# Two gated blocks between linear-attention layers: the first gated block opens with row tiles 0 and 1 in one group, and the five engine orders are written anew

## The chip, the cores and the metric

The kernel runs as one program on one core of a Trainium2 chip. The metric is the device time of one execution in microseconds (us). Seven executions of the kernel before gave 379.11 to 379.82 us, median 379.69 us.

## The reference

The input x has 2048 rows of 512 bf16 numbers. Four blocks follow one another, each with a layer norm in front and a residual sum behind it: A (attention), B (gated), A again, B again, with the same weights in both rounds.

```
A(x):  q, k, v = x @ wqkv, 32 heads of 16
       phi(t) = [softmax(t @ w_phi), softmax(-(t @ w_phi))]   # per head, 16 + 16 features
       kv = sum over rows of phi(k)^T v ;  z = sum over rows of phi(k)
       o  = phi(q) kv / (phi(q) z + 1e-6) ;  result o @ wo
B(x):  gate = x @ W_gate ; up = x @ W_up        # 512 -> 1376
       result (relu(gate) * up) @ W_down        # 1376 -> 512
x = x + A(norm(x)); x = x + B(norm(x)); x = x + A(norm(x)); x = x + B(norm(x))
```

The sum over all rows in kv is the one place where no row can go on until every row is done. Everything else goes row tile by row tile.

## The kernel before

The rows are cut into 16 tiles of 128. x stays on chip as `x_sb`. The blocks have the tags A0, B1, A2 and B3, and the layer norms in front of them L0 to L3.

**Attention.** For a tile t the names are: `k t` and `v t` (projection matmuls, line 725, or 766 for pairs of tiles), `expk` (two exponentials on ScalarE), `Zk` (a row reduction on VectorE), `rZk` (its reciprocal), `phik` (the scaling, on GpSimd or VectorE), and `kvacc` (line 787), which adds into PSUM banks 0 and 1. After the last tile, `kvbd` and `kvf` (lines 797 and 808, VectorE) take kv out of these two banks. Then, for each tile, comes the numerator: for tiles 0 and 1, and 10 to 15, of A0, `num` is eight small matmuls (line 921), `rden` and `o` on VectorE. For tiles 2 to 9 of A0 (line 886) the eight products of 144 columns go to PSUM in three groups, `numcp t 0`, `t 1`, `t 2` evacuate them (line 413, ScalarE or VectorE), and `zm`, `zd`, `zr`, `ab`, `tsc` and `o` do the division. The three groups take banks 6 and 7 in turn. `otr` transposes `o` (on TensorE with an evacuating copy for tiles 0 and 1, by a DMA on SyncE's queue for the others). `wo t` is the output projection (line 942, four matmuls), `resid` adds it to x (line 687, VectorE), `apply` centres the row for the next norm (line 703), and `L1 tr t` transposes it into `yT` (TensorE plus copy for tiles 0 and 1, a DMA else). The query projections stand as `q 6 2` and so on (line 868: four tiles at a time, transposed) or `q 12` (line 822), each with exponentials `expq`. The exponentials of a pair of tiles are two ScalarE instructions over two banks.

**Gated block.** `glu_up` takes a group of row tiles `ts` and walks over 11 chunks of the 1376 columns. For each of ten full chunks, `Wg` and `Wu` (line 962) make four matmuls each: the weights' chunk stands in the array, and `yT` of the group streams through it, so that a matmul has 128 columns for each tile in the group. `relu` (line 964) brings the gate out of PSUM on ScalarE; in every second chunk `up` (line 970) brings the other product out on ScalarE too and `h` (line 972) multiplies on VectorE, in the others `h` (line 975) reads PSUM itself. The last chunk, of 96 columns, is done the other way about (`gu`, line 988, four matmuls of 192 columns for each tile, with `h` line 993) and comes first; its product goes through a DMA transpose (`htr`). The products of gate and up go round banks 0 to 3, which the query projections used before. `glu_down` (line 1011) is eleven matmuls of 512 columns per tile, and its `resid` (line 1013) adds to x.

**The order of the work.** `emit` lists the operations; each has a number. The dictionary `ORDER` holds, for each of the five engines, the numbers in base 36 in the order in which that engine runs them; nothing decides this at run time. `CHOICE` says on which engine an operation runs that more than one could do. Semaphore waits are derived from the operations' reads and writes. The durations written beside the operations only help to sort the operations when waits are shared out. SyncE issues all transposes and most weight loads in the order of its list, and an issue that waits holds up those behind it. `dummy` (line 539) stands for 70 matmuls without use, spread over the first part of TensorE's list.

In the first gated block the groups are: tile 0, tile 1, tiles 2 and 3, tiles 4 to 7, 8 to 11, 12 to 15. In the second one they are: tiles 0 and 1, tiles 2 and 3, and then the same fours.

Of the kernel before, what the change touches and what calls it, by code (L numbers as in the profile page):

```python
# [14 lines left out]
        "29 26 6 25 27 28 2a 2b 4t 2c 39 49 3u 4y 4e 44 5i 5n 58 5s 4j 6j 6k 67 73 72 8l 6d 84 6a 4o 83 8k 91 9x 9y 7r 96 9z c4 c5 9b c6 9g d9 da db b4 f9 f8 "  # L15
        "fm fl ay ee ef b2 eg gz gy fz h0 hx hw fy ij g5 g4 ik gb ga gg gh ii hv mk mj n4 n3 mu mt lm lq lt ne nd nn no nt r8 o5 o4 rf of op oq jv kn p0 pa pb "
        "vg pl pw pv vk q6 qg qh qr s1 ko sd sc sn xw xt sx sy t8 lg tt tj ti zn u4 ue u3 zu up uo uz wd wo wp x9 wz xa m8 ru ym yn xk z7 11o z8 yx 10k 11s zi "
        "10l 11v 10v 142 w2 12t yb 149 146 134 13p 135 13f 109 159 14z 13q 15a 15u 12a 15v 15k 14o 16x 178 177 17i 1b7 16m 18l 1aw 1c9 1db 1ad 1by 1d0 1e6 1dv "
        "1ea 1f0 1fg 1ew 1em 1gj 1fw 1gk 1fc 1gi 1jm 1hk 1hl 1hj 1kb 1fs 1ib 1ic 1kr 1l7 1g8 1ia 1j2 1j3 1gx 1ll 1lk 1j1 1m9 1ma 1nv 1k6 1ob 1mz 1my 1lj 1or "
        "1l3 1kn 1p7 1nn 1m8 1mn 1no 1mx 1pl 1pk 1ly 1q9 1nm 1o7 1nc 1qa 1pj 1qz 1qy 1on 1rq 1rp 1q8 1s4 1p3 1qx 1s3 1py 1ro 1t5 1t6 1s5 1s6 1t8 1qn 1t7 1u7 "  # L20
        "1ua 1u8 1xr 1uw 1uv 1u9 1xx 1y3 1uy 1ym 1yn 1ux 1z1 1z2 1y9 1yl 1zh 1zg 1z0 1zv 1zw 1zf 24t 1zu 24u 255 24v 24w 256 258 230 257 25u 25t 25h 25i 25k "
        "25w 25v 25j 26q 271 27d 272 22j 27n 27c 27z 27o 27y 289 28a 28l 28k 28v 28w 297 29h 296 29i 29t 29s 2be 23c 23x 2bp 2bq 24i 2cc 2cb 2c1 26f 2c0 2dj "
        "2cn 2cm 2di 2dt 2b3 2e5 2du 2e4 2ef 2eg 2er 2eq 2ft 2fu 2hu 2i5 2i6 2ih 2ig 2j2 2ir 2j3 2a7 2is 2d7 2kg 2k6 2kh 2k5 2l2 2l3 2ks 2kr 2mh 2le 2mg 2ld "
        "2fi 2hb 2ju 2m5 2qa 2pz 2qb 2n8 2ql 2qw 2qx 2qm 2sa 2r7 2sl 2sb 2r8 2ny 2sw 2sx 2t7 2sm 2pg 2t8 2um 2tj 2ti 2ul 2g8 2rz 2mv 2ua 2vw 2x5 2ak 2v0 2xg "
        "2xr 2xh 2od 2y3 2xs 2y2 2vd 2yd 2yp 2ye 2yo 2z0 2zb 2yz 2zm 2za 2zl 2gl 2wo 2zw 2zx 308 2wb 307 30z 2oq 31c 30m 322 "),
    "dve": (
        "2z 30 33 3a 3b 3e 3l 3m 3v 3k 3w 3p 2m 53 3z 5d 5x 5z 5t 5v 5u 60 5y 5w 7i 7g 7f 7h 6l 64 6m ao 74 ap 75 an am 85 7t 86 8m a0 7x 8n 7v a3 a1 a4 c7 ca "
        "c8 cb dc df b0 fa dg fn dd fo fb eh ek el ei em h1 h2 fq h4 hy hz h5 i1 il im i0 in io j2 j1 j3 j4 ix jd iz je iy j0 k6 jj k7 ku ky l1 l2 jo l3 l4 jp "
        "l6 l7 lv lw ju kc ly lz nu kh rc rg ki rh og ld ri o6 le or p1 rk pc pm rl vn vo q7 m5 px vq qi m6 xp qs kp s2 vs so se r4 sz xy xz t9 rr tk tu y1 u5 "
        "uf uq zr 13s we lh v0 zw zx zy zz rs vc 13t vz x0 wq w0 y8 y9 xb yo xl 13v 106 107 17w yy 15x zj 15y m9 z9 17x 15z 10m 17y 1b9 1ba 19o 10w 12u 11y 181 "  # L30
        "19p 14c 120 121 136 118 14d 13g 16c 14e 16d 150 19r 1cb 127 11k 13r 15b w3 128 1cc 18b 18c 15w 15l 1cd 14l 14m 16y 16j 16k 17j 179 17v 18i 18j 1a3 1a4 "
        "1bo 1bp 19b 1cq 1cr 18z 1aa 1ab 1b8 1dl 1ax 1dm 19n 1bv 1cx 1bw 1cy 1ca 1e8 1ds 1dt 1e7 1eb 1dc 1ey 1fe 1f3 1fh 1d1 1en 1ex 1jk 1kp 1fu 1fx 1gl 1fj "
        "1ft 12b 1k9 1fd 1l8 1ks 1gy 1dw 1hm 1g9 1hn 1j4 1j5 1gm 1id 1ha 1go 1nt 1l5 1nw 1mb 1ie 1i1 1hp 1mc 1la 1o9 1is 1k7 1jj 1p5 1oc 1gn 1os 1op 1ko 1p8 "
        "1lm 1ln 1n0 1ig 1n1 1n2 1l4 1lo 1pm 1lz 1lp 1nd 1np 1mo 1j7 1nq 1pn 1po 1r0 1pp 1r1 1o8 1r3 1qb 1qc 1s7 1s8 1oo 1p4 1rr 1rs 1se 1sf 1pz 1qo 1t9 1tg "
        "1rf 1xp 1ta 1th 1qe 201 1xs 1sw 1xv 202 203 20f 1xu 1ty 1tl 204 20g 1y1 208 209 1yo 1um 1y7 1y6 1yp 1z3 1ya 1yq 1z4 1yc 1zi 1zj 1zl 1zx 1zy 200 1zz "
        "20a 21r 21q 21s 21p 20d 221 222 227 22u 22v 22c 23n 23o 22d 20m 22i 248 249 235 236 265 23b 20n 2et 26r 266 2gm 2eu 24f 23u 23v 273 2ev 27e 2gn 280 "
        "28b 27p 2at 24g 2au 28m 2go 2lg 298 2cx 29j 28x 29u 2cy 2j5 26c 2j6 26d 2n9 2na 2f8 2f9 2bf 23d 2a6 2lh 2br 2aj 2li 2ll 2b0 2h1 2cd 2c2 2h2 2d4 2ff "
        "2co 23y 2b1 2or 2os 2dk 2nc 2d5 2fg 2e6 2eh 2dv 2es 2tl 2fv 2jk 2jl 2g7 2ra 2ou 2b4 2hv 2rb 2i7 2ow 2lv 2tm 2lw 2gk 2it 2h8 2h9 2ii 2j4 2no 2m2 2k7 "
        "2np 2rf 2m3 2jr 2js 2l4 2ki 2kt 2p6 2p7 2lf 2mi 2mu 2rp 2nv 2nw 2rq 2n7 2m6 2u0 2u1 2qc 2q0 2hc 2jv 2op 2oc 2vm 2pd 2qn 2qy 2pe 2r9 2sc 2rw 2rx 2vn "
        "2t9 2sn 2sy 2tk 2un 2uz 2u7 2u8 2vt 2vu 2vc 2x6 2xt 2ub 2xi 2wa 2yf 2wn 2y4 2yq 2s0 2zn 2z1 2zy 2zc 309 30l 30y 31b 31o 320 "),  # L40
# [375 lines left out]
class Kernel:  # L416
# [609 lines left out]
    def emit(self):  # L1026
# [45 lines left out]
        for li in (0, 2):  # L1072
# [52 lines left out]
            else:  # L1125
                for f in steps_B([0], HA):
                    f()
# [86 lines left out]
```

The softmax here doesn't subtract the row's maximum and nothing guards it: scores larger than these inputs give would overflow.

## Time and profile before

| what | value |
|---|---|
| seven executions | 379.11 to 379.82 us, median 379.69 us |
| the profiled execution's own time | 379.33 us |
| its span, first to last instruction | 377.2 us |
| TensorE busy (matmuls) | 368.0 us, 98% of the span |
| VectorE, ScalarE, GpSimd busy | 276.1, 226.9, 130.6 us |
| granted TensorE clock | 1.000 |

The time of the profiled execution is its span and 2.1 us around it. Busy time of TensorE counts a matmul from its start to its modelled end, and matmuls overlap: a 512-column matmul is shown with 379 ns, while four of them in a row take 0.86 us in the chain, a pace of 0.216 us each. So the pace, and not the mean duration, says what a matmul costs in a full queue.

### The profile page before, as it was taken

To read this page: it belongs to the slowest core of one execution; us is meant where nothing else is said; L and a number is where in the kernel's file an instruction comes from. 1 tells how busy PE (TensorE), PEld (TensorE's weight loads), DVE (VectorE), ACT (ScalarE), POOL (GpSimd) and SP (SyncE) were. 2 spreads that over 40 slices of the span, in tenths; PEclk is the share of its full clock that TensorE was granted. 3 is DMA by queue.
4 is the path that set the end of the run, shared out by engine and by line. 5 is a ranking of instruction groups with operands and counts; after the bars stand their busy time and mean duration, and the time that the engine had idled before them with its cause. 6 is when DMAs were issued, how large, how long until landed. Compare 5 with 4: busy or idle time off the path is not lost.

```text
span 377.2 us, 6882 instructions
## 1 busy us (share of the span) xinstructions
PE 368.0 (98%) x2519; PEld 204.3 (54%) x2565; DVE 276.1 (73%) x607; ACT 226.9 (60%) x463; POOL 130.6 (35%) x234
## 2 busy tenths in 40 slices
PE   6999999999999999999999999999999999999997
PEld 5654555877744454454444446577664454445443
DVE  5999998989968666559899999888984654342323
ACT  3999878765744127874677568584635451653450
POOL 7799941132344001350463577023221201000020
PEclk9999999999999999999999999999999999999999
DMA  7742893313425434310300044435443342142012
GB/s 236 171 81 49 194 247 137 75 33 57 78 44 98 98 59 83 70 30 14 71 0 1 3 82 88 85 63 101 77 84 80 76 89 52 28 71 70 30 42 70
DMA packets 87856, 29.33 MB, mean 78 GB/s; under 512 B 79792, under 2 KB 86800, under 8 KB 87824
## 3 DMA queue, kind: packets, MB, share of 16 engines
q1 hardware_dynamic: 84368, 25.86, 33.2%
q10 hardware_dynamic: 3456, 3.05, 2.5%
q8 instruction: 20, 0.33, 0.3%
q14 instruction: 12, 0.10, 0.1%
HBM read 7.91 MB, written 2.10 MB: 27 GB/s over the span
## 4 chain that ended last, share of the span: by engine, by line
PE 84%; POOL 7%; DVE 3%; issue 2%; ACT 1%; DMA 1%; SPq 0%; POOLq 0%; DVEq 0%
PE ps L962 37%; PE ps L1011 20%; PE ps L725 7%; PE ps L942 7%; POOL expk L750 5%; PE ps L822 5%; PE ps L988 3%; PE ps L921 2%; DMA x_sb<-in_A_x_dram 1%; PE ps L787 1%; PE ps L886 1%; DVE Zk L744 1%; POOL rstd L648 1%; PE ps L868 1%; DVE expk L755 0%
## 5 line engine op out<-in xcount | busy, mean ns | idle before, releaser
L962 PE MATMUL ps<-yT,Wgu 128*128 128x512 bf16 (+2 forms) x870 | 150.8, 320 | 0.6
L962 PEld LDWEIGHTS ps<-yT,Wgu 128*128 128x128 bf16 x880 | 78.5, 98 | 58.8 <-ACT expk L970 1.0
L964 ACT ACTIVATE gate_sb<-ps 128x512 bf16<-128x512 f32 (+2 forms) x110 | 50.7, 480 | 55.1 <-PE ps L962 41.8
L1011 PE MATMUL ps<-Wd,hT 128*128 128x512 bf16 (+4 forms) x354 | 79.3, 373 | 0.5
L1011 PEld LDWEIGHTS ps<-Wd,hT 128*128 128x128 bf16 (+1 forms) x363 | 34.7, 98 | 39.4 <-DVE hT L972 0.7
L972 DVE TENSOR_TENSOR hT<-gate_sb,expk 128x512 bf16<-128x512 bf16 (+2 forms) x70 | 23.9, 360 | 30.4 <-ACT expk L970 21.4
L970 ACT ACTIVATE expk<-ps 128x512 bf16<-128x512 f32 (+2 forms) x70 | 32.0, 475 | 22.3 <-PE ps L962 19.6
L710 ACT ACTIVATE sq<-x_sb,nmr 128x512 bf16<-128x512 bf16 x48 | 34.6, 721 | 10.3 <-DVE x_sb L687 6.6
L744 DVE TENSOR_REDUCE Zk<-expk 128x64 f32<-128x1024 bf16 x32 | 38.1, 1203 | 1.0 <-ACT expk L737 0.7
L714 POOL TENSOR_TENSOR rstd<-rv,mone 128x1 f32<-128x1 f32 x32 | 18.6, 587 | 50.3 <-DVE rv L712 50.0
L1013 DVE SCALAR_TENSOR_TENSOR x_sb<-ps,rstd,x_sb 128x512 bf16<-128x512 f32 (+2 forms) x33 | 23.9, 728 | 16.2 <-PE ps L1011 13.5
L942 PE MATMUL ps<-wo_p,oT 128*128 128x512 bf16 x118 | 30.8, 379 | 0.6 <-DVE oT L413 0.3
L975 DVE TENSOR_TENSOR hT<-gate_sb,ps 128x512 bf16<-128x512 bf16 (+2 forms) x40 | 21.7, 544 | 12.7 <-ACT gate_sb L964 6.4
L855 POOL TENSOR_TENSOR expq<-expq,rho 128x256 bf16<-128x256 bf16 x36 | 22.1, 622 | 24.4 <-DVE rho L852 23.6
L847 DVE TENSOR_REDUCE Zq<-expq 128x64 f32<-128x1024 bf16 x24 | 28.8, 1203 | 0.8 <-POOL rho L852 0.5
L687 DVE SCALAR_TENSOR_TENSOR x_sb<-ps,x_sb 128x512 bf16<-128x512 f32 x32 | 21.9, 687 | 8.7 <-PE ps L942 7.8
L750 POOL TENSOR_TENSOR expk<-expk,rZk 128x1024 bf16<-128x1024 bf16 x13 | 25.9, 2007 | 0.6 <-DVE rZk L746 0.6
L755 POOL TENSOR_TENSOR expk<-expk,rZk 128x512 bf16<-128x512 bf16 x17 | 19.0, 1131 | 11.8 <-DVE rZk L746 11.6
L822 PE MATMUL ps<-Wqp,yT 128*128 128x512 bf16 x91 | 22.8, 379 | 0.3
L725 PE MATMUL ps<-Wkp,yT 128*128 128x512 bf16 x84 | 22.0, 379 | 0.2
L725 PE MATMUL ps<-wv_p,yT 128*128 128x512 bf16 x85 | 21.9, 379 | 0.2
L712 POOL TENSOR_SCALAR rv<-rv 128x1 f32<-128x1 f32 x22 | 4.3, 203 | 45.3 <-ACT sq L710 45.3
(126 smaller groups left out, 514.1 us busy)
## 6 DMA issues: line engine op xcount, KB each, us to landing
out_dram<-x_sb ACTq DMA_DIRECT2D x15, 128.0 KB, 1.7
x_sb<-in_A_x_dram SPq DMA_DIRECT2D x3, 512.0 KB, 5.7
Wgu<-in_B_W_up_dram SPq DMA_DIRECT2D x4, 344.0 KB, 5.2
Wgu<-in_B_W_gate_dram SPq DMA_DIRECT2D x4, 344.0 KB, 4.2
Wd<-in_B_W_down_dram SPq DMA_DIRECT2D x5, 256.0 KB, 3.2
yT<-ytile SPq DMA_TRANSPOSE x56, 2.5
qT<-expq SPq DMA_TRANSPOSE x40, 2.5
hT<-in_A_wqkv_dram ACTq DMA_DIRECT2D x4, 128.0 KB, 4.3
```

Source lines behind the costliest of these rows:

```text
L710: op("act", lambda e: e.activation(k.sq[:], k.x_sb[:, t, :], ACT.Square, scale=-float(D), bias=k.nmr[:, t, :], accum_out=k.rv1[:, t, :]), ...
L725: op("pe", (lambda ic, bank, W: lambda e: e.matmul(k.pb[bank][:], k.yT[:, ic, t * 128:(t + 1) * 128], W[:, ic, :], start=(ic == 0), stop=( ...
L744: op("dve", lambda e: e.tensor_reduce(k.Zk[:, zb, :], k.expk[:, t, :, :, :].rearrange("p g s (h f) -> p (g s h) f", f=16), AX.X, ALU.add), ...
L750: op("pool", lambda e: e.tensor_tensor(kv, kv, k.rZk[:, rb, :].unsqueeze(2).to_broadcast([P, 64, 16]), ALU.mult), [r("expk", t, 0), r("exp ...
L822: op("pe", (lambda ic, bank, tt: lambda e: e.matmul(k.pb[bank][:], k.yT[:, ic, tt * 128:(tt + 1) * 128], k.Wqp[:, ic, :], start=(ic == 0), ...
L847: op("dve", lambda e: e.tensor_reduce(k.Zq[:, b, :], k.expq[:, t, :, :, :].rearrange("p g s (h f) -> p (g s h) f", f=16), AX.X, ALU.add), ...
L942: op("pe", (lambda c, bank: lambda e: e.matmul(k.pb[bank][:], k.oT[:, ob, c, :], k.wo_p[:, c, :], start=(c == 0), stop=(c == NC - 1)))(c, ...
L962: op("pe", (lambda bank, W, ic, fc, Mf: lambda e: e.matmul(k.pb[bank][0:Mf, 0:n], W[:, ic, fc * 128:fc * 128 + Mf], k.yT[:, ic, c0:c0 + n] ...
L964: op("act", (lambda Mf, gb, gs: lambda e: e.activation(k.gate_sb[0:Mf, gs, 0:n], k.pb[gb][0:Mf, 0:n], ACT.Relu))(Mf, gb, gs), [self.RP[gb] ...
L970: op("act", (lambda Mf, ub, up: lambda e: e.activation(up[0:Mf, 0:n], k.pb[ub][0:Mf, 0:n], ACT.Copy))(Mf, ub, up), [self.RP[ub]], ru, 170 ...
L972: op("dve", (lambda Mf, up, gs, u: lambda e: e.tensor_tensor(k.hT[0:Mf, u, 0:n], k.gate_sb[0:Mf, gs, 0:n], up[0:Mf, 0:n], ALU.mult))(Mf, u ...
L1011: op("pe", (lambda fc, Kf, u, c0, bank, m0, m1: lambda e: e.matmul(k.pb[bank][:, m0:m1], k.hT[0:Kf, u, c0:c0 + 128], k.Wd[0:Kf, fc, m0:m1] ...
```

## The change

One group of tiles 0 and 1 takes the place of the groups of tile 0 and of tile 1 in the first gated block; the second block already had it. In line with that all five lists of `ORDER` are replaced, and `CHOICE` moves some 95 operations to another engine. The code that counts:

```diff
-            if last:
-                mix(steps_B([0, 1], HA), steps_N([4]))
-            else:
-                for f in steps_B([0], HA):
-                    f()
-                mix(steps_B([1], HA), steps_N([4]))
+            mix(steps_B([0, 1], HA), steps_N([4]))
...
-        op("act", lambda e: e.activation(k.sq[:, 0:1], ones_c[:, 0:1], ACT.Exp), [r("ones")], [r("sq"), r("tbl")], 1450, "table")
+        op("act", lambda e: e.activation(k.sq[:, 0:1], ones_c[:, 0:1], ACT.Exp), [r("ones")], [r("sq"), r("tbl")], 250, "table")
...
-            self.op2("act" if on_act else "dve", apply, dep, dst, {"dve": 407, "act": 825}, f"{tag} apply {t}", 250.0)
+            how = CHOICE.get(f"{tag} apply {t}", "act" if on_act else "dve")
+            other = "act" if how == "dve" else "pool" if t < 9 and how == "act" else "dve" if how == "act" else "act"
+            dd = {"dve": 407, "act": 825, "pool": 2090}
+            self.op2(how, apply, dep, dst, {e: dd[e] for e in (how, other)}, f"{tag} apply {t}", 250.0)
...
```

The number 1450 or 250 and the dictionary `dd` are planning durations and change no instruction. The counts follow from the code: TensorE loses 80 matmuls of line 962 (160 of 128 columns become 80 of 256). With the moves by `CHOICE`, the lists go from 2565 to 2485 operations on TensorE, from 438 to 424 on ScalarE, from 559 to 550 on VectorE, from 230 to 226 on GpSimd and from 171 to 170 on SyncE (one `htr` less).

The lists, with the numbers read back into names, differ at these places that matter for what follows ("x4" is four matmuls; a part of a list each, in order):

```
TensorE before: num 1 (4..7); otr 0; num 1 (0..3); q 6 2; q 6 3; num 2 x8; wo 0; num 3 (0..3); q 12; num 3 (4..7);
                q 13; q 14; q 15; L1 tr 0; otr 1; num 4 (0..3); gu 0; wo 1; Wu 0 1; Wu 0 0; Wg 0 0; num 4 (4..7);
                Wg 0 1; Wu 0 2; Wg 0 2; wo 2; Wg 0 3; L1 tr 1; ...
TensorE after:  num 1 x8; otr 0; q 6 2; num 2 (0..3); q 6 3; num 2 (4..7); wo 0; num 3 (0..3); q 14; q 12; num 3 (4..7);
                otr 1; q 13; L1 tr 0; num 4 (0..3); q 15; wo 1; num 4 (4..7); gu 0; num 5 (0..3); L1 tr 1; wo 2;
                Wu 0 0; gu 1; Wg 0 0; Wu 0 1; Wu 0 2; Wg 0 2; Wg 0 1; ...
VectorE before: o 0; kvf; kvf; rden 1; otr 0 copy; o 1; numcp 2 0; ... tsc 3; o 3; h 0 10; resid 1; numcp 4 1; zm 4; apply 1
VectorE after:  o 0; kvf; kvf; rden 1; o 1; otr 0 copy; numcp 2 0; ... tsc 3; resid 1; numcp 4 2; apply 1; zm 4; o 3; zd 4;
                L1 tr 1 copy; zr 4; h 0 0; h 0 10; h 0 1; tsc 4; h 0 2; resid 2; h 0 3; apply 2; h 0 4; zm 5; h 0 5; resid 3;
                h 0 6; zr 5; ab 5; h 0 7; tsc 5; apply 3; o 5; h 0 9; h 0 8; ...
ScalarE before: numcp 3 0, 3 1, 3 2; expq 12 1, 12 0; expq 14 0, 14 1; relu 0 10; numcp 4 0; up 0 0; relu 0 0; numcp 4 2
ScalarE after:  numcp 3 0; L1 var 0; numcp 3 1, 3 2; otr 1 copy; expq 12 0; numcp 4 0; expq 12 1; numcp 4 1; expq 14 1, 14 0;
                up 0 0; numcp 5 0; relu 0 0; relu 0 10; ...
SyncE before:   dma Wd1 ahead of otr 2; dma Wd3 behind otr 2
SyncE after:    otr 2; otr 3; dma Wd4; dma Wd3; htr 0; dma Wd1; otr 4; ...
Front, VectorE before: stats 2; aggr 2; stats 3; ytrcopy 1; aggr 3; apply 2; BD; wtrcopy wk 1; apply 3; wtrcopy wk 2; stats 6
Front, VectorE after:  stats 2; nrx 0; aggr 2; BD; stats 3; aggr 3; apply 2; ytrcopy 2; apply 3; wtrcopy wk 2; stats 6
Front, ScalarE before: ytrcopy 0; vcopy 0; ytrcopy 2; compcopy wk 0; vcopy 1; ...
Front, ScalarE after:  ytrcopy 0; ytrcopy 1; vcopy 0; compcopy wk 0; wtrcopy wk 1; vcopy 1; ...
Front, VectorE, a little later: before stats 10; Zk 0; apply 4        after stats 10; apply 4; Zk 0
```

In these front names, `stats`, `aggr`, `apply`, `ytrcopy` and `nrx` belong to L0 (lines 623 to 679), `BD` is line 560, and `wtrcopy` and `compcopy` are the evacuations that prepare the key weights (line 413, called from lines 588 and 592).

## The prediction

> **What bounds the kernel now.** First the page's busy times, then the table of stretches, then who TensorE waits for, then the chain of waits.
>
> ```profile
> PE 368.0 (98%) x2519; PEld 204.3 (54%) x2565; DVE 276.1 (73%) x607; ACT 226.9 (60%) x463; POOL 130.6 (35%) x234
> ```
>
> TensorE is busy 98% of the span: the kernel is bound by its queue, and what the other engines do counts only where TensorE waits for them. The stretches (length, then busy time of PE, PEld, DVE, ACT, POOL, clock, DMA) show where that is near:
>
> ```profile
> 14.00:52.00 38.00, 37.73 (x285) 19.65 (x289) 37.51 (x54) 36.36 (x56) 35.64 (x41) 1.00 0.56 111
> 52.00:57.00 5.00, 4.51 (x62) 2.76 (x60) 4.82 (x13) 2.82 (x4) 0.00 (x0) 1.00 0.94 318
> 57.00:66.00 9.00, 8.30 (x59) 4.67 (x59) 7.33 (x19) 7.19 (x10) 1.49 (x3) 1.00 0.37 126
> 66.00:90.00 24.00, 23.74 (x269) 18.58 (x274) 22.03 (x67) 15.32 (x54) 7.21 (x14) 1.00 0.25 48
> 90.00:205.00 115.00, 114.42 (x632) 58.25 (x643) 86.63 (x187) 67.11 (x141) 36.99 (x72) 1.00 0.30 56
> ```
>
> From 14 to 52 us all four engines are full; from 52 to 66 us TensorE lacks 1.2 us; the first gated block's opening (66 to 90) has VectorE at 22.0 of 24 us; then TensorE never lacks work. The waits of TensorE after the start are few:
>
> ```profile
> PE ps L886 <- DVE expk L413: 0.5, 1, 0.5
> PE ps L942 <- DVE oT L413: 0.3, 1, 0.3
> PE ps L868 <- DVE qT L808: 0.2, 1, 0.2
> PE ps L921 <- DVE kvbd L797: 0.2, 1, 0.2
> ```
>
> The chain gives the pace of matmuls in a full queue (start, us, what, how many in a row):
>
> ```profile
> 9.09 0.05 issue
> 9.14 0.40 PE ps L678 x4
> ...
> 11.11 0.69 ACT vsb L730
> ...
> 60.96 0.86 PE ps L822 x4
> ...
> 71.75 0.89 PE ps L962 x16
> ...
> 252.39 4.37 PE ps L962 x40
> ```
>
> That is 0.0556 us for 128 columns, 0.109 for 256, 0.216 for 512 (0.083 for the 192 of `gu`, 0.0625 for the 144 of `num`, from other such rows). I laid these paces along TensorE's list and took the sum from the traced start of each weight load. What is left is the wait gathered so far, "the lag": 5.9 us at 14.4 us, 6.7 at 52.4, 8.6 at `wo 0` (59.6), 9.1 at the first matmuls of B1 (67.1), 9.4 at 205.8, 10.6 at the end; the paces alone sum to 366.2 us. No list can win more than a part of the 2.4 us that fall between 52.4 and 67.1, the 0.5 beside 205 to 226 and the 0.8 at 236 to 241, or of the front. For the new lists I add the same paces for each instruction's place and follow by hand the producers at the hand-overs, with durations from this trace.
>
> **The change, part by part.**
>
> *Matmuls.* 160 x 0.0556 = 8.9 us become 80 x 0.109 = 8.7; `gu` stays 8 of 192 columns. Gain 0.15 us, all on the path, bounds 0 and 0.3 by the rounding of the rows. The groups' mean durations (219 and 273 ns) would say 35.0 against 21.8 us, but they are mostly overlapped latency. The Trainium skill ("TensorE: Matmul & The Clock Gate", Back-to-back issue gap) gives about 81 ns per matmul of 128 columns in a real stream of weight loads; by that the 160 would take 13.0 us and pairing would win some 4 us. The row of 16 in 0.89 us contradicts it here, and the sum goes by the row.
>
> *Evacuations.* ScalarE: 20 `relu` of 277 ns and 10 `up` of 276 become 10 of 381 and 5 of 382, and two of 265 one of 345: 8.8 us become 6.1. VectorE: 10 `h` of 274, 10 of 232, two of 242 become 5 of 418, 5 of 308, one of 344: 5.5 become 4.0. I count nothing: TensorE's queue of 23.7 us covers both (22.0 and 15.3 us); without that cover it is a gain of up to 1.5 us on VectorE, held in the range's low end.
>
> *Front, to 53 us.* Before tile 2's `apply`, VectorE's new list has `BD` (684 ns) and `nrx 0` (139), which came later or ran on GpSimd, and lacks a `yT` copy (401): `L0 ytr 2` comes at 9.6 instead of 9.14 us. On ScalarE `wtrcopy wk 1` (0.5 us of pitch) enters the gapless row that starts at 11.11, while the `yT` copy of tile 2 leaves ahead of it; the copy of tile 1 falls into ScalarE's idle 6.9 to 8.3 us. `expk 0` ends 0.3 us later, and VectorE fills that with `apply 4`, which now stands ahead of `Zk 0`. Against it, VectorE's own work up to `kvbd` shrinks by 0.3 us (two copies of about 0.4 leave, one copy and `nrx` come). So `kvbd` comes between 0.3 us earlier and 0.45 later; I take 0.2 later, nearer the chain because all engines are full to 52 us.
>
> *The first numerators, 53 to 60 us.* `num 2`'s first four now stand ahead of `q 6 3`. TensorE reaches them at 57.6 us and waits until `o 1` frees banks 6 and 7 (`rden 1` ends 57.1, 0.69 us for `o 1`: 57.8), 0.2 us. But the first cast of `num 2` can run at 58.2 instead of 58.9, so the last two products, which waited the 0.5 us of line 886, find their bank free at 59. The lag at `wo 0` becomes 8.2 instead of 8.6: gain 0.4, bounds 0 and 0.5.
>
> *The opening of B1, 60 to 69 us.* Before, tile 0's chunks filled TensorE between `wo 1` (65.9) and `L1 tr 1` (69.5). Now nothing full-size of B1 may start before tile 1 is in `yT`. The sum of paces ahead of `wo 1` is 56.6; with 8.2 it runs from 64.8 to 65.6 and is out at 65.8. Behind it stand `num 4`'s last four, `gu 0`, `num 5`'s first four (0.25 + 0.33 + 0.25 = 0.8 us), then `L1 tr 1`. VectorE is in `tsc 3` (1.21) until about 66.05, then `resid 1` 0.69, the cast `numcp 4 2` 0.45, `apply 1` 0.34: 67.55. On ScalarE the `expq 12` pair (1.02 each) starts behind `q 13` and `otr 1 copy` at 63.85, with `numcp 4 0` (0.53) between: 66.3, then `numcp 4 1` 66.8. Hence `gu 0`, whose bank held `q 12`, waits 0.4 us; `num 5` waits for the banks until 66.85 and, for its fourth, 67.25; `L1 tr 1` starts at 67.6, `wo 2` covers 0.86, the copy of tile 1 (0.40) comes behind `zm 4`, `o 3` and `zd 4` and ends near 68.9. The first 256-column matmul has place 59.3: lag 9.55, where before it was 9.1 at that point. From 8.2 to 9.55 is 1.35 against 0.5 before: a loss of 0.9 us, bounds 0 (ScalarE and VectorE half a us ahead) and 1.5.
>
> Behind it VectorE waits: `h 0 0` stands first and needs `relu 0 0` (70.8), `h 0 1` needs `relu 0 1` (72.45), some 2.5 us idle. Following the list (`tsc` 1.21, `resid` 0.69, `h` 0.31 or 0.42), `h 0 8` ends at 81.2, and `down 0` (place 70.0) reads it at 81.3. That is no loss, and no margin.
>
> *Queues.* SyncE issues `Wd1` (256 KB, 3.2 us to landing) behind `otr 3` and `htr 0`, at some 73 us: landed by 77, read by `down 0` at 80. `tr 2` and `tr 3` (2.5 us) land by 82.8, read at 83.6. GpSimd has 7.2 us in 24 here; the `o` and `ab` taken from it add 1.7 us to VectorE, and the `numcp` given to ScalarE take off 1.8 net.
>
> *The rest.* The lists from 90 to 205 us keep pairs of hand-overs as far apart (`wo 7` to the first `Wg 4`: 5.05 us of places for 3.8 us of `resid`, `apply` and transpose). At 226 to 245 us I find 0.35 us before `num 0` and 0.45 before `num 1`, and none before `wo 0`, against 0.8 before. Zero, bounds 0.7 gain (these waits go) and 1.0 loss (as much again as the last 170 us hold now).
>
> *Sum:* -0.15 - 0.4 + 0.9 + 0.2 = +0.55 us. On the profiled execution's 379.33 that is 379.9; that execution lies 0.36 below the median of the runs, 379.69, so for a median I take 380.1. The bound for no change, 0.2%, is 0.76 us (about what a measurement of this kernel can tell from no change): 378.93 to 380.45.
>
> **The rivals.**
>
> *The opening does not wait* (faster). If ScalarE runs half a us ahead of my count, `expq 12` and the casts are out before TensorE asks, and `resid 1` finds VectorE free. For it: in the profile ScalarE is idle 0.8 us at 57.9 and 0.5 at 61.5. Against it: `resid 1` to `apply 1` alone is 1.5 us against 0.8 us of cover. With 0.9 gone and the front 0.3 earlier: -0.85, or -1.3 with half of the later waits: 378.6.
>
> *VectorE sets B1's start* (slower). `down 0` waits for `h 0 8`; from the point where VectorE's lag grows by more than 0.1 us every further us counts, with two `tsc` of 1.21 us in that stretch. One `tsc` late, on top of the sum, gives 381.4. For it: 22.0 of 24 us busy before, and the 2.5 us of idle that the new list forces. Against it: 1.5 us less of `h`, and `numcp` to ScalarE.
>
> *`Wd1` is late* (slower). If `htr 0` is held 3 us, the load lands behind `down 0`'s third matmul; 2 us gives 382. The DMA share of 0.25 speaks against it.
>
> **How the numbers follow.** No measurable change, 380.1: 0.40. VectorE 0.30 and `Wd1` 0.06: slower 0.36. Faster 0.24. The range reaches to both, 378.4 to 381.9, leaving about 0.1 on each side; the likeliest case alone has 379.0 to 380.4.
>
> **What would show it.** Right: 80 more matmuls of 256 columns at 0.109 us and none of 128 at line 962; the wait of line 886 on a cast gone; a wait of line 988 or 697 for ScalarE or VectorE at 66 to 68 us; the first 256-column matmul near 69 us; lag 9.5 there and again at 205. Wrong: waits of line 1011 for `hT` or `Wd` near 80 us, a `kvbd` more than half a us off 52.9, or a new wait in the A2 stage.

## The result and the profile after

The changed kernel takes 381.3 us (median of 16 executions, 379.58 to 382.88); the kernel before, beside it, 379.46 us (41 executions, 378.93 to 380.34). The ratio is 1.0044, with a 95% interval of 1.0034 to 1.0054: slower by 1.8 us. Beside the loss there is a spread of 3.3 us, where the kernel before has 1.4. The profiled execution of the changed kernel, 380.29 us with a span of 378.4, lies in the lower part of that spread, so the two traces differ by 1.0 us only.

In the changed kernel some line numbers are one or two away from those of before: the matmuls of gate and up are line 963, `apply` of L0 is 661 on VectorE and 660 on ScalarE, `kvbd` 798, `phik` 751, `kvacc` 788. In the experiments they move by a few more.

The busy times, then the same stretches as before (length, then PE, PEld, DVE, ACT, POOL, clock, DMA):

```profile
PE 367.5 (97%) x2441; PEld 201.4 (53%) x2485; DVE 274.7 (73%) x598; ACT 226.0 (60%) x449; POOL 127.9 (34%) x230
```

```profile
14.00:52.00 38.00, 37.00 (x266) 18.56 (x270) 37.44 (x52) 36.11 (x55) 35.36 (x40) 1.00 0.43 86
52.00:57.00 5.00, 4.75 (x68) 3.04 (x68) 4.87 (x13) 1.94 (x2) 0.21 (x1) 1.00 0.89 247
57.00:66.00 9.00, 8.65 (x69) 4.80 (x68) 8.16 (x22) 7.56 (x12) 0.30 (x1) 1.00 0.55 195
66.00:90.00 24.00, 23.61 (x189) 16.93 (x191) 19.67 (x50) 16.60 (x41) 6.01 (x13) 1.00 0.36 77
```

The first line is the one that moved against us: from 14 to 52 us TensorE lacks 1.0 us, where before it lacked 0.27. From 52 to 66 us it lacks 0.6 instead of 1.2. In the opening VectorE has gone from 22.0 to 19.7 of 24 us, and TensorE lacks 0.4 as against 0.26. The waits of TensorE:

```profile
PE ps L679 <- DVE ytile L671: 1.0, 1, 1.0
PE ps L922 <- DVE osb L929: 0.4, 1, 0.4
...
PE ps L943 <- DMA oT<-osb: 0.3, 1, 0.3
PE ps L767 <- DMA yT<-ytile: 0.3, 1, 0.3
PE ps L726 <- DMA yT<-ytile: 0.2, 1, 0.2
```

New are the two waits of key projections for transposed tiles (lines 767 and 726, `k 12` at 40.7 us and `k 14` at 45.1) and the wait of line 922 at 239.9 us (`num 1` of A2). The wait of line 886 on a cast, 0.5 us before, is gone. In the chain:

```profile
38.20 2.51 DMA yT<-ytile
...
42.41 2.65 DMA yT<-ytile
...
69.62 0.44 PE ps L963 x4
...
70.39 2.64 PE ps L963 x24
```

The last line gives 0.110 us for each of 24 matmuls of 256 columns. The two DMA lines are the transposes that TensorE waits for.

To place the loss I take the measure of the prediction, the wait that TensorE has gathered above the sum of its paces, for every profile of this study, and cut it at five points: the first transpose of tile 2 (`L0 ytr 2`), the sixth product of `num 0`, the last of `num 2`, `L1 tr 1`, and the end (us).

| kernel | to `L0 ytr 2` | to `num 0` | to `num 2` | to `L1 tr 1` | to the end | all |
|---|---|---|---|---|---|---|
| before | 5.47 | 1.90 | 1.25 | 0.48 | 1.59 | 10.69 |
| changed | 5.69 | 2.84 | 0.64 | 0.93 | 1.84 | 11.94 |
| e1 changed again | 5.73 | 2.92 | 0.64 | 0.94 | 1.82 | 12.05 |
| e12 changed again | 6.10 | 2.84 | 0.64 | 0.93 | 1.90 | 12.41 |
| e2 old front | 5.56 | 1.90 | 0.63 | 0.95 | 2.20 | 11.24 |
| e3 old tail | 5.55 | 3.29 | 0.63 | 0.95 | 1.83 | 12.25 |
| e4 `tr 14` first | 6.20 | 2.73 | 0.63 | 0.95 | 1.82 | 12.33 |
| e5 `apply 13` early | 6.09 | 2.09 | 0.64 | 0.94 | 1.83 | 11.59 |
| e6 and `phik 14` late | 5.65 | 2.88 | 0.63 | 0.94 | 1.86 | 11.96 |
| e7 before, `apply 13` late | 5.34 | 3.04 | 2.37 | 0.41 | 1.74 | 12.90 |
| e8 before, `num 2` split | 5.16 | 1.93 | 0.81 | 1.26 | 1.89 | 11.05 |
| e9 opening alone | 5.34 | 1.94 | 0.64 | 0.94 | 2.60 | 11.46 |
| e10 `phik 7` in two | 5.93 | 3.31 | 0.64 | 0.94 | 1.84 | 12.66 |
| e11 `phik 7`, `12` in two | 5.90 | 2.00 | 0.64 | 0.94 | 1.69 | 11.17 |

The paces themselves sum to 366.2 us for the list of before and to 366.0 for the changed one. The second column of numbers holds the loss: 1.9 us with the front of before, 2.7 to 3.3 in seven of the kernels with the new front, and back to 2.0 and 2.1 in e11 and e5. (e7, with 3.04, has the front of before with one exchange in it.) Each row is one profiled execution.

### The profile page after: what moved, and what is told of

Read it like the earlier page. It is cut to its first block, busy times and chain, and to the rows that moved or that the text cites. A ratio compares the mean times of both kernels' runs of the same rounds, so it can differ in the third digit from the quotient of the medians.

```text
span 378.4 us, 6684 instructions
## 1 busy us (share of the span) xinstructions
PE 367.5 (97%) x2441; PEld 201.4 (53%) x2485; DVE 274.7 (73%) x598; ACT 226.0 (60%) x449; POOL 127.9 (34%) x230
## 4 chain that ended last, share of the span: by engine, by line
PE 86%; DVE 4%; ACT 4%; DMA 4%; issue 1%; SPq 0%
PE ps L963 36%; PE ps L1012 19%; PE ps L726 10%; PE ps L943 7%; PE ps L823 3%; PE ps L989 2%; PE ps L788 2%; PE ps L767 2%; PE ps L922 1%; ACT expk L770 1%; DMA yT<-ytile 1%; DMA x_sb<-in_A_x_dram 1%; DMA oT<-osb 1%; PE ps L869 1%; PE ps L887 1%
## 5 line engine op out<-in xcount | busy, mean ns | idle before, releaser
L963 PE MATMUL ps<-yT,Wgu 128*128 128x512 bf16 (+1 forms) x788 | 149.0, 336 | 0.7 <-issue 0.2
L963 PEld LDWEIGHTS ps<-yT,Wgu 128*128 128x128 bf16 x800 | 75.6, 98 | 59.4 <-ACT expk L971 1.5
L1012 PE MATMUL ps<-Wd,hT 128*128 128x512 bf16 (+3 forms) x353 | 79.0, 372 | 0.6
L965 ACT ACTIVATE gate_sb<-ps 128x512 bf16<-128x512 f32 (+1 forms) x100 | 50.1, 510 | 46.4 <-PE ps L963 38.1
L971 ACT ACTIVATE expk<-ps 128x512 bf16<-128x512 f32 (+1 forms) x65 | 31.6, 497 | 28.1 <-PE ps L963 14.7
L973 DVE TENSOR_TENSOR hT<-gate_sb,expk 128x512 bf16<-128x512 bf16 (+1 forms) x65 | 22.6, 363 | 26.8 <-ACT expk L971 14.5
L713 POOL TENSOR_SCALAR rv<-rv 128x1 f32<-128x1 f32 x30 | 6.7, 231 | 94.4 <-ACT sq L711 94.4
L976 DVE TENSOR_TENSOR hT<-gate_sb,ps 128x512 bf16<-128x512 bf16 (+1 forms) x35 | 20.8, 598 | 13.2 <-PE ps L963 6.5
L756 POOL TENSOR_TENSOR expk<-expk,rZk 128x512 bf16<-128x512 bf16 x18 | 20.2, 1129 | 14.4 <-DVE rZk L747 13.6
```

Source lines behind the costliest of these rows:

```text
L963: op("pe", (lambda bank, W, ic, fc, Mf: lambda e: e.matmul(k.pb[bank][0:Mf, 0:n], W[:, ic, fc * 128:fc * 128 + Mf], k.yT[:, ic, c0:c0 + n] ...
L965: op("act", (lambda Mf, gb, gs: lambda e: e.activation(k.gate_sb[0:Mf, gs, 0:n], k.pb[gb][0:Mf, 0:n], ACT.Relu))(Mf, gb, gs), [self.RP[gb] ...
L971: op("act", (lambda Mf, ub, up: lambda e: e.activation(up[0:Mf, 0:n], k.pb[ub][0:Mf, 0:n], ACT.Copy))(Mf, ub, up), [self.RP[ub]], ru, 170 ...
L1012: op("pe", (lambda fc, Kf, u, c0, bank, m0, m1: lambda e: e.matmul(k.pb[bank][:, m0:m1], k.hT[0:Kf, u, c0:c0 + 128], k.Wd[0:Kf, fc, m0:m1] ...
```

## Where the front loses it: one instruction of VectorE

VectorE reaches `kvbd` at 52.86 us before and at 53.95 (first of four) after. I set VectorE's instructions up to there against each other, name by name. The largest difference by far is one instruction, `L0 apply 13`, which centres and scales row tile 13. The timeline of before, VectorE and then GpSimd (start, length, what):

```profile
33.63 1.21 DVE L744 TENSOR_REDUCE Zk<-expk 128x64 f32<-128x1024 bf16 x1
34.76 0.95 DVE L663 TENSOR_SCALAR ytile<-x_sb,rstd,nmr 128x512 bf16<-128x512 bf16 x1
...
52.86 0.98 DVE L797 TENSOR_TENSOR kvbd<-ps,mask 128x136 bf16<-128x136 f32 x4
...
33.63 3.86 POOL L750 TENSOR_TENSOR expk<-expk,rZk 128x1024 bf16<-128x1024 bf16 x2
```

And after:

```profile
33.92 1.21 DVE L745 TENSOR_REDUCE Zk<-expk 128x64 f32<-128x1024 bf16 x1
35.05 1.89 DVE L661 TENSOR_SCALAR ytile<-x_sb,rstd,nmr 128x512 bf16<-128x512 bf16 x1
36.86 0.54 DVE L747 RECIPROCAL rZk<-Zk 128x64 f32<-128x64 f32 x1
...
53.95 1.05 DVE L798 TENSOR_TENSOR kvbd<-ps,mask 128x136 bf16<-128x136 f32 x4
...
32.98 3.81 POOL L751 TENSOR_TENSOR expk<-expk,rZk 128x1024 bf16<-128x1024 bf16 x2
```

What matters is when the first of the two GpSimd instructions gives way to the second (`phik 6 0` to `phik 7 0`, each some 1.93 us). Before, that is at 35.5 us; `apply 13` comes at 34.76, towards the end of `phik 6 0`, and is out 0.15 us after its end. After, the hand-over is at 34.9 us; `apply 13` comes at 35.05, 0.2 us behind the start of `phik 7 0`, and is out 0.15 us after that one's end, at 36.94. The same instruction for tile 10 takes 0.31 us before, beside a small GpSimd instruction (`rstd 12`, a few columns), and 0.71 after, where it comes during `phik 3 0` and is out 0.15 us after its end at 29.19 (before, VectorE and GpSimd; then after):

```profile
26.98 0.31 DVE L663 TENSOR_SCALAR ytile<-x_sb,rstd,nmr 128x512 bf16<-128x512 bf16 x1
...
26.73 1.01 POOL L648 TENSOR_TENSOR rstd<-rv,mhalf 128x4 f32<-128x4 f32 x1
```

```profile
28.64 0.71 DVE L661 TENSOR_SCALAR ytile<-x_sb,rstd,nmr 128x512 bf16<-128x512 bf16 x1
```

The reduction `Zk` takes 1.21 us whatever GpSimd does. So the theory (G): an `apply`, or a `phik` on VectorE, that is issued while such a GpSimd instruction runs waits until that one instruction ends; the new front shifts the two engines by a few tenths of a us against each other, and `apply 13` falls from the end of one GpSimd instruction to the start of the next. One rival is that VectorE is late because of the order of its own instructions, another that ScalarE's stores at the end set the time.

The Trainium skill ("SBUF — State Buffer", Who interferes with whom) states a rule for this: a VectorE instruction in a mode that uses both of its port pairs, or one with two inputs in SBUF against a GpSimd instruction that reads SBUF, contends with GpSimd for one shared port pair, and whichever is issued first holds it for its whole instruction. The rows above agree with it, with 0.15 us from the release to the end of `apply 13`.

## The experiments

The expectations of e1 to e4 were written before theory G; their theories are that the front (F), the opening (O) or the tail (T) carries the loss. G was written down after them and is put to the test from e5 on.

**e1: the changed kernel again.** No edit beyond the lists being written out anew.

> The changed kernel once more, as the common yardstick. All theories: 381.3 us median, 1.8 above the kernel before; TensorE's gathered wait again 7.8 us before kvbd (6.7 in the kernel before) and 10.1 at the first 256-column matmul. Theory F (the front: key projections of tiles 6, 9, 12 and 14 wait for their transposes) says that these four waits come back within 0.3 us. Theory T (the tail: the stores of tiles 12, 13 and 7 stand behind the store of tile 14) says that the time outside the span varies by more than a us.

380.9 us (five executions, 380.78 to 381.4), ratio 1.0043 (1.0031 to 1.0055): the loss is the kernel's and not that of one measurement. In its trace `apply 13` takes 1.95 us.

**e2: the front of before.** All five lists up to `kvbd` are those of before; everything behind is as changed.

```diff
-all five engines, up to kvbd: the changed order
+all five engines, up to kvbd: the order of before
 behind it: the changed order (opening with tiles 0 and 1, and all the rest)
```

> The changed kernel, with everything up to kvbd in the order and on the engines of the kernel before. Theory F: the waits for the yT transposes go, the gathered wait before kvbd is 6.7 us instead of 7.8, time 381.3 - 1.2 = 380.1 us. Rival O (the opening of the first gated block carries the loss): 381.0 to 381.3. Theory T: 381.3, or 380.1 with the same spread between executions.

379.35 us, ratio 0.9999 (0.9989 to 1.0008). The whole loss is gone, and so is the spread (379.04 to 379.66 in eleven executions). The timeline of VectorE has the lines of before again:

```profile
34.85 0.95 DVE L660 TENSOR_SCALAR ytile<-x_sb,rstd,nmr 128x512 bf16<-128x512 bf16 x1
...
52.94 0.98 DVE L797 TENSOR_TENSOR kvbd<-ps,mask 128x136 bf16<-128x136 f32 x4
```

So the opening, the first numerators, the long stretch and the tail together cost nothing in time that can be told from zero. The new order of the stores is among them, so the tail (T) is not the cause. The equal times hide a small difference: the span is 0.3 us longer than that of before (medians 377.4 and 377.1 us) and the time around it as much shorter (1.9 and 2.2), which no run explains.

**e3: the end of ScalarE's list as before.** The change had put the stores of tiles 13 and 7 behind that of tile 14, whose data come late.

```diff
 ScalarE, end:
-store 10; store 14; store 12; store 13; store 7; store 15
+store 10; store 13; store 7; store 14; store 12; store 15
```

> The changed kernel with one change on ScalarE's list: the stores of tiles 13 and 7 ahead of that of tile 14, as in the kernel before. Theory T: the last store lands 0.2 us earlier in the span and the varying part outside the span goes: about 380.5 us and a narrower spread. Theories F and O: 381.1 to 381.3.

380.44 us (379.24 to 383.52), ratio 1.0036 (1.0018 to 1.0055). The median is near the 380.5 us that theory T named, but the intervals of e1 and e3 overlap, the spread grew where T had it shrink, and e2 has the new tail without the loss. So this is not the cause. Its trace taught more than its time. Here `apply 13` came just ahead of the hand-over and took 0.41 us, and the waits of `k 12` and `k 14` for transposes were gone; but 13 us later `phik 14 0` on VectorE came 0.05 us behind the start of GpSimd's `phik 12 0`:

```profile
48.50 2.42 DVE L755 TENSOR_TENSOR expk<-expk,rZk 128x512 bf16<-128x512 bf16 x1
```

In the changed kernel's own trace `phik 14 0` comes 0.16 us ahead of `phik 12 0` and takes 0.74 us, and there GpSimd's instruction is the longer one, 2.38 instead of 1.93 us:

```profile
49.68 0.74 DVE L756 TENSOR_TENSOR expk<-expk,rZk 128x512 bf16<-128x512 bf16 x1
...
49.84 2.38 POOL L751 TENSOR_TENSOR expk<-expk,rZk 128x1024 bf16<-128x1024 bf16 x1
```

In e3 the 1.7 us show as a wait of 1.4 us of `kvacc 15` for the features that VectorE writes behind it. The front thus has two places where a tenth of a us decides over 1 to 1.7 us.

**e4: `tr 14` ahead of a weight load.** If the wait of `k 14` for its transpose is a cause by itself, an earlier issue on SyncE removes it.

```diff
 SyncE:
-L0 tr 15; dma wo1; L0 tr 14; dma Wd2
+L0 tr 15; L0 tr 14; dma wo1; dma Wd2
```

> The changed kernel with the transpose of tile 14 ahead of the load of wo1 on SyncE's list (the load waits until tile 15's transpose has landed). Theory F: the 0.4 us at the key projection of tile 14 goes, 380.9 us. Rivals O and T: no change, 381.3.

381.16 us, ratio 1.0055 (1.0038 to 1.0071): no gain. The wait of `k 14` went and `kvacc 15` waited 0.3 us longer instead; `apply 13` took 2.02 us. Over all profiles the waits of `k 12` and `k 14` follow `apply 13`. Where it takes 1.89 us or more, TensorE's gathered wait grows at these two by some 0.8 us together (changed, e1, e12), and by 0.4 at `k 12` alone in e4; in the five other traces with the new front it does not grow there. SyncE issues `tr 13` ahead of `tr 12` and `tr 14`, so a late `apply 13` holds those too.

**e5: `apply 13` one place earlier.** In the changed kernel, VectorE.

```diff
 VectorE, front:
-Zk 8; Zk 9; apply 13; rZk 9
+Zk 8; apply 13; Zk 9; rZk 9
```

> The changed kernel with one instruction moved: apply 13 of L0 goes ahead of Zk 9 on VectorE's list. Theory G (a VectorE instruction on bf16 tiles in SBUF and a GpSimd instruction shut each other out, so apply 13, which starts 0.1 us after the 1.92 us of GpSimd's phik 7 0, takes 1.9 us): it now meets the second half of phik 6 0, takes about 1.0 us, kvbd comes 0.9 us earlier, and the time is near 380.0 us where the changed kernel has 380.9 to 381.3; the spread stays, since phik 14 0 still starts within 0.1 us of GpSimd's phik 12 0. Rival W (the waits of the key projections for their transposes are the cause): unchanged, 381, because the transposes behind tile 13's on the queue are no earlier.

379.94 us (379.49 to 381.25), ratio 1.0018 (1.0009 to 1.0026): more than half of the loss is back with one exchange. `apply 13` takes 1.26 us, kept by the last 1.1 us of `phik 6 0`, and the stretch up to `num 0` holds 2.09 us of waits instead of 2.84 to 2.92.

**e6: both places moved.** On top of e5, `phik 14 0` leaves the neighbourhood of `phik 12 0`.

```diff
 VectorE, front:
-rZk 14; phik 14 0; Zk 15; rZk 15; phik 14 1
+rZk 14; Zk 15; rZk 15; phik 14 0; phik 14 1
```

> As the run before, and phik 14 0 moved behind Zk 15 and rZk 15 on VectorE's list, so that it no longer starts together with GpSimd's phik 12 0. Theory G: 379.8 us, and a spread as narrow as that of the kernel before (0.7 us), since neither of the two meetings can go the bad way. Rival W: 381, spread unchanged.

380.49 us, ratio 1.003 (1.002 to 1.0041): a miss, 0.7 us above what G gave. In its trace `apply 13` waited again, 1.59 us, because it came 0.5 us after the start of `phik 6 0`, and `phik 14 0` at its new place still took 1.09 us, out 0.55 us after the end of `phik 12 0` at 51.71. I had moved two meetings and not removed them.

**e7: the kernel before, made to meet.** The same exchange in the kernel before, where by the trace it puts `apply 13` at the start of `phik 6 0` (33.6 us).

```diff
 VectorE, front of before:
-Zk 8; Zk 9; apply 13; Zq 0
+Zk 8; apply 13; Zk 9; Zq 0
```

> The kernel before with apply 13 moved ahead of Zk 9 on VectorE's list, where it meets the start of GpSimd's phik 6 0. Theory G: it takes 1.9 us instead of 0.95, though its transpose leaves at the same time; kvbd comes up to 1.0 us later and the time goes from 379.4 to 380.3 us. Rival W: no change, 379.4.

380.91 us (380.77 to 381.71), ratio 1.0046 (1.0034 to 1.0059): one exchange of neighbours in the old list, without any part of the change, costs as much as the whole change. The direction is G's; the size is larger than the 0.9 us that I had put down.

```profile
33.51 2.09 DVE L663 TENSOR_SCALAR ytile<-x_sb,rstd,nmr 128x512 bf16<-128x512 bf16 x1
```

The stretch up to `num 0` goes from 1.90 to 3.04 us. The further 1.1 us in this profile fall between `num 0` and `num 2`, where the granted clock (third from the right in a row) fell to a half:

```profile
52.00:55.00 3.00, 2.02 (x37) 1.50 (x37) 3.00 (x9) 1.62 (x2) 0.19 (x1) 1.00 0.77 242
55.00:58.30 3.30, 3.08 (x10) 1.15 (x11) 2.56 (x6) 0.00 (x0) 0.00 (x0) 0.51 1.01 336
```

This profiled execution has the longest span of its kernel, 379.4 us; the other four, with the clock at 1.0, have 378.7, still 1.6 above that of before (377.1). Where the 0.5 us beyond the meeting lie in those four no trace shows.

**e8: `num 2` split, in the kernel before.** The step on which the prediction put its gain of 0.4 us, done alone.

```diff
 TensorE, before:
-q 6 2; q 6 3; num 2 (0..7); wo 0
+q 6 2; num 2 (0..3); q 6 3; num 2 (4..7); wo 0
 VectorE, before:
-rden 1; otr 0 copy; o 1
+rden 1; o 1; otr 0 copy
```

> The kernel before with one part of the new lists: num 2's first four matmuls ahead of q 6 3 on TensorE, and the copy for otr 0 behind o 1 on VectorE. By the prediction's sum the gathered wait at wo 0 falls from 8.6 to 8.2 us and the time by 0.4, to 379.0 us; if the opening of the first gated block gives it back by waiting for VectorE, 379.4.

379.9 us, ratio 1.0012 (1.0004 to 1.0021): a miss. The wait of `num 2` went as argued (0.81 us from `num 0` to `num 2` instead of 1.25), and the next one took its place:

```profile
PE ps L822 <- ACT expq L871: 0.6, 1, 0.6
```

`q 12` is now reached at 60.9 us and needs the banks that `expq` of `q 6` empties at 60.86. In the changed list `q 14` stands ahead of `q 12`, and that wait is absent. So the split wins only together with the order behind it.

**e9: the opening alone.** The regrouped opening and the order about it from 53 to 99 us, between the lists of before on both sides.

```diff
 up to kvbd:         the order of before
+53 to 99 us:        the changed order, tiles 0 and 1 in one group
 from 99 us on:      the order of before
```

> The regrouped opening of the first gated layer, and the order around it from 53 to 99 us, between the order of the kernel before up to kvbd and the order of the kernel before from 99 us on. Theory (the regroup itself costs nothing that can be seen; the loss is made in the front, where apply 13 comes behind a GpSimd instruction): the sum of TensorE's waits is 6.8 us at the last kvacc 15, 1.6 more through the first numerators, 0.6 in the opening as in the second run, and 1.6 from there to the end as before; matmuls 0.2 less; a span 0.1 to 0.4 under that of before, 378.9 to 379.4 us, ratio 0.999 to 1.000. Rival (the opening with two tiles costs what the prediction put on it, 0.9 us, and the order of the rest in the changed kernel made up for it): 379.9 us or more.

379.61 us (378.79 to 380.19), ratio 0.9999 (0.999 to 1.0008): the ratio that the theory gave, and 0.3 us under the rival's time. In time, the regrouping as such neither wins nor loses. As in e2, the span is longer (377.8 against 377.4 us, medians) and the time around it shorter (1.8 against 2.3). In the trace 0.6 us are won from `num 0` to `num 2`, 0.45 lost up to `L1 tr 1`, 0.27 at `Wu 2 9` (98.4 us), where the two orders meet, and 0.67 at `wo 12` (136 us), which waited for its transpose where before it did not. Between the two places where the orders meet, the opening gains some 0.35 us, the 0.2 of the matmuls included; the last two waits lie at and behind the second of them:

```profile
PE ps L943 <- DMA oT<-osb: 0.5, 1, 0.5
```

My count for the last two, nothing, was wrong; the rival's price of 0.9 us for the opening was not seen either.

**e10: `phik 7 0` in two pieces.** A test of G that moves nothing: the orders are those of the changed kernel, and the work is the same.

```diff
-op("pool", lambda e: e.tensor_tensor(kv, kv, rZk, ALU.mult), ...)
+def norm(e):                       # rZk stands for the broadcast of k.rZk[:, rb, :]
+    if t == 7:
+        e.tensor_tensor(kv[:, 0:32, :], kv[:, 0:32, :], rZk[0:32], ALU.mult)
+        return e.tensor_tensor(kv[:, 32:64, :], kv[:, 32:64, :], rZk[32:64], ALU.mult)
+    return e.tensor_tensor(kv, kv, rZk, ALU.mult)
+op("pool", norm, ...)
```

> The changed kernel with all five orders as they are; only GpSimd's phik 7 0 is issued as two instructions of 32 groups each instead of one of 64. Theory (an apply on VectorE that meets a GpSimd instruction waits for that one instruction's end): apply 13 waits for the first half alone and lasts 0.8 to 1.1 us instead of 1.9, kvbd begins 0.8 to 1.0 us earlier, TensorE's waits from ytr 2 to num 0's last product fall from 2.9 to about 2.1 us, and the time is 0.6 to 0.8 us less than the changed kernel's, about 380.2 us. Rival (VectorE is late because of the order of its own instructions, and the long apply 13 is a symptom): apply 13 lasts 1.9 us as before, and the time is the changed kernel's, 380.9 us or more.

380.28 us (379.52 to 382.42), ratio 1.0025 (1.001 to 1.004): the median as theory G put it. Eight of eleven spans lie between 377.6 and 377.9 us, three at 379.1, 379.2 and 380.5. The profiled execution is of the three, and shows the other meeting, VectorE first and then GpSimd (`phik 13 0` and `phik 12 0`, the second from 48.85 us):

```profile
48.88 2.44 DVE L761 TENSOR_TENSOR expk<-expk,rZk 128x512 bf16<-128x512 bf16 x1
...
46.96 3.81 POOL L755 TENSOR_TENSOR expk<-expk,rZk 128x1024 bf16<-128x1024 bf16 x2
```

Its `apply 13` took 0.45 us, since it came ahead of the end of `phik 6 0`; so this profile says nothing on the half instruction, and its `kvbd` was late, against the expectation.

**e11: `phik 7 0` and `phik 12 0` in two pieces.**

```diff
-    if t == 7:
+    if t in (7, 12):
```

> The run before, with GpSimd's phik 12 0 cut into two instructions as well; orders as in the changed kernel. Theory (the long times of the run before, three of eleven with a span over 379 us, are those in which VectorE's phik 14 0 came a few hundredths of a us behind the start of GpSimd's phik 12 0 and waited 1.7 us, as in its profile, and the others those in which it came ahead of it): now such a meeting costs 0.9 us at most. The median stays where it was or falls a little, 380.0 to 380.3 us; no span is over 378.9 us. Rival (the spread has another source): one run in four still has a span over 379 us.

379.98 us, ratio 1.0015 (1.0005 to 1.0025); all twelve spans between 377.6 and 378.4 us. Here the profiled execution has the meeting that the changed kernel has, with the short instruction (VectorE, then GpSimd):

```profile
34.06 1.21 DVE L745 TENSOR_REDUCE Zk<-expk 128x64 f32<-128x1024 bf16 x1
35.19 1.08 DVE L661 TENSOR_SCALAR ytile<-x_sb,rstd,nmr 128x512 bf16<-128x512 bf16 x1
...
33.18 1.92 POOL L755 TENSOR_TENSOR expk<-expk,rZk 128x1024 bf16<-128x1024 bf16 x1
35.06 1.05 POOL L753 TENSOR_TENSOR expk<-expk,rZk 128x512 bf16<-128x512 bf16 x1
36.08 1.10 POOL L754 TENSOR_TENSOR expk<-expk,rZk 128x512 bf16<-128x512 bf16 x1
```

`apply 13` comes 0.13 us behind the start of the first half, at 35.19, and is out at 36.27, 0.16 after that half's end at 36.11. With the uncut instruction it is kept as long as that one runs: 1.89, 1.95, 2.02 and 2.03 us in four traces. Orders and work are the same, and 0.8 to 0.95 us on VectorE and 0.84 us on TensorE (2.84 to 2.00) are gone. This rules out that VectorE's own order makes `apply 13` long. The two runs e11 and e12 stand side by side: 379.98 us with the instructions cut, 380.95 without.

**e12: the changed kernel, beside e11.**

> The changed kernel as it is, beside the run with both instructions cut, for its spread. Theory: spans from 377.6 us (neither meeting) over 378.5 to 379 (one) to 380.5 (both), median near 378.7; time near 381.0 us.

380.95 us (379.68 to 382.48), ratio 1.0035 (1.0023 to 1.0048). Three of its spans are 377.3 to 377.8 us, nine 378.6 to 379.1. The two groups are as expected for the first two cases, though no execution of the shorter group was profiled; the third (380.5) did not come here. In the other measurements of kernels with the new front, the spans of 380.2 us and more are four, and each has a mean clock of 0.995 or 0.996. So that group is more likely the clock of e7 than both meetings at once; this is argued and not shown, since none of the four was profiled.

## Why the prediction was right or wrong

It named 380.1 us as likeliest, with no measurable change as the likeliest case; measured is 381.3, slower by 0.44%, inside its range and outside the likeliest case. The 380.1 is also not what its own sum gives: 379.69 and 0.55 make 380.24. That the time lies inside the range is luck, for the range reaches so high because of two slower rivals, and neither of them happened: `Wd1` was issued at 73.1 us and nothing waited for it, and `h 0 8` ended at 81.7 us with no visible wait of `down 0`.

- *Matmuls, -0.15.* The paces of the two lists differ by 0.22 us. Right, as far as the rows show: 24 in 2.64 us is 0.110 us each, where 0.109 was counted.
- *Front, +0.2 (bounds -0.3 and +0.45).* This is the step that failed. Up to `num 0` the gathered wait grew by 1.16 us in the traces compared (7.37 to 8.53), and by 1.6 in e12. Its first half was right: `L0 ytr 2` was put at 9.6 us and came at 9.36 in the changed kernel's trace and between 9.21 and 9.86 in all nine traces with the new front. But VectorE's work up to `kvbd` was then summed by the durations of the trace of before, as if they belonged to the instructions, and `kvbd` was put between 0.3 earlier and 0.45 later; it came 1.1 later. The trace of before held the warning: `apply 13` with 0.95 us stood beside an `apply 10` with 0.31. Of the signs that the prediction listed against itself, `kvbd` more than half a us off came true, and it points at the cause. A new wait in the A2 stage, 0.4 us at `num 1`, came true as well; the count had named it, and e2 has it without the loss.
- *First numerators, -0.4.* They won 0.6 us from `num 0` to `num 2`, and the wait on the cast is gone. Right in reason, and a little more than counted. What the count does not say is that the gain needs the order behind it: e8 shows that the split alone hands the wait on to `q 12`.
- *Opening, +0.9.* Measured is 0.45 (0.93 against 0.48). The waits are where they were put: 0.24 us at `gu 0` (0.4 named), 0.3 at `num 5`'s fourth, 0.2 at `L1 tr 1`; each a little shorter. From the end of `num 2` to there the count had 1.35. The first 256-column matmul is at 69.6 instead of 68.9 us, mostly because of the front.
- *Rest, 0.* Plus 0.25 us: 0.24 at `wo 12`, and the wait before `num 1` of A2 is 0.56 (0.45 named).
- *The sum.* With the measured terms, +1.08 up to `kvacc 15`, -0.53 to `num 2`, +0.45, +0.25 and -0.22 make 1.03 us, and the two profiled executions differ by 0.96. The median differs by 1.8 because the profiled execution is among the shorter ones. Part of that stays open, see below.

What the change says it does, the regrouping, is worth nothing in time either way (e9); what made it slower is the front, written along with it (e2), and for more than half of the loss it is a shift of a few tenths of a us there, by which `apply 13` meets a long GpSimd instruction (e5, e11). Some 0.5 us of the loss stays in e5 and e11 (379.94 and 379.98). By the traces the likeliest place is the later `L0 ytr 2`, 5.55 to 6.20 us of waits to there with the new front against 5.16 to 5.56 with the old; no run changed that alone. No version tried beats the kernel before; e2 and e9 equal it.

## What to carry to other kernels

Before summing an engine's work for a new order, look for instructions of one shape whose durations differ in the trace: the longer ones may hold a wait, and here it went with the neighbour on the other engine, not with the instruction. Where VectorE and GpSimd work side by side, lay their timelines over each other and ask which of them starts first at each meeting, and by how much; a margin of 0.1 us there falls one way in one execution and the other way in the next. Here, cutting the long GpSimd instruction halved the price without touching any order, for 0.2 us more of GpSimd's time. Moving the VectorE instruction by one place won 1.0 us in one list (e5), lost 1.5 in another (e7), and a second move on top of the first won nothing more (e6).

## What the runs showed of the hardware

- The same VectorE instruction (`apply` of a tile, 128 by 512) took 1.26, 1.59, 1.89 and 2.09 us beside a 1.93 us GpSimd instruction of 1024 columns, always out 0.15 us behind that instruction's end; and a GpSimd instruction that began 0.16 us behind `phik 14 0` took 2.38 us. It is a wait for the whole instruction, in both directions; with the GpSimd instruction cut in two it is a wait for one half, 1.08 us. Beside `rstd 12`, which GpSimd's row shows for 1.0 us, `apply 10` took 0.31 us and did not wait; why that one holds nothing is open.
- In e7 the granted clock fell to 0.51 from 55 to 58.3 us, right after 3 us in which TensorE was busy for 2.0. The four executions with a mean clock of 0.995 and 0.996 elsewhere have spans of 380.2 to 380.5 us. The Trainium skill ("TensorE: Matmul & The Clock Gate", What's actually happening) has the clock at a half after an idle window of some 3.4 us; here no window of that length was idle, only a third of one. A third without work is not enough by itself either: in e3 and e10 TensorE was busy for 1.6 of the same 3 us, and the clock stayed at 1.00. What brought it down in e7 is open.
- Open: in some executions of the kernels with the new front the time around the span is 2.7 to 4.2 us (six of 17 of the changed kernel), where the kernels with the front of before have 1.7 to 2.4. No run was made on it. It is the upper end of the changed kernel's spread.
